# Depthwise convolution on tiles of the TensorE array, with channels copied across by GpSimd

## The chip, the cores and the metric

The kernel runs on one core of a Trainium2 chip. The metric is the device time of one execution in microseconds. [...] Each engine takes its instructions in the order of the program, so one that waits holds up all behind it on its engine.

## What is computed

Attention over a window of 32 positions to either side, for 8 batches of 8 heads with 576 positions and a head size of 64, and then a feed-forward part whose hidden layer gates itself by a convolution along the sequence.

```python
def _attn_ref(q, k, v):                      # (8, 8, 576, 64) each
    scores = scale * np.matmul(q, k.transpose(0, 1, 3, 2))
    mask = np.abs(pos[:, None] - pos[None, :]) <= 32
    scores = np.where(mask, scores, -1000000000.0)
    ...                                      # softmax
    return np.matmul(attn, v)

def _moe_ref(x, w_in, conv_w, w_out):        # x (8, 576, 512), w_in 512x1024, conv_w 3x1024
    h = np.maximum(x @ w_in, 0.0)
    hp = ...                                 # one row of zeros at either end of the sequence
    for k in range(3):
        conv_out += conv_w[k][None, None, :] * hp[:, k:k + S, :]
    gate = 1.0 / (1.0 + np.exp(-conv_out))
    return h * gate @ w_out                  # float32, (8, 576, 512)
```

The convolution is depthwise: each of the 1024 channels has three weights of its own and sees only itself.

## The kernel before

All matmul operands are bf16. The feed-forward part works with channels on partitions, in 12 chunks `c` of 384 positions (two thirds of a sequence) and 8 blocks `m` of 128 channels. For one block of one chunk the steps are: projection (`ph_mm`, 4 matmuls of 385 or so columns, the outer columns being the neighbours that the convolution needs), ReLU on ScalarE from PSUM into `hT` (`relu`), convolution, tanh on ScalarE in PSUM (`tanh`; the sigmoid is written with it), and the gate on VectorE (`gate`), which adds 1, multiplies by `hT` and writes `gT`. After a chunk's eight blocks come three groups of output matmuls (`py_mm`, 8 of 512 columns each), a copy on ScalarE and a store. Chunks 0 and 1 go in halves of 192 columns.

The convolution of a block is made in one of three ways, by tables (`ON_POOL`, `ON_DVE`, lines 1017 to 1029, `conv_by`). On TensorE (`pc_mm`) it is three matmuls, one a tap, with a 128x128 diagonal matrix of weights (`diag_w`) as the stationary operand and `hT` shifted by a column as the moving one; they add up in one PSUM bank. On VectorE (`conv_acc`) ScalarE makes the first tap into PSUM and VectorE adds the other two. On GpSimd (`conv_pool`) it is five operations in SBUF (`ca`, `cb`), and the tanh then reads SBUF. In chunks 2 to 11 the tables give 10 blocks to GpSimd, 43 to VectorE and 27 to TensorE.

The attention of batch `b` runs ahead of the chunks that need it. Per batch: loads of q, k, v in float32; casts to bf16 on GpSimd (`cast_qk`, `cast_v`); q and k turned so that the head dimension lies on partitions, by nine 128x128 transposes on TensorE for half of the heads (`tr_mm`, copied out of PSUM by ScalarE and VectorE in two parts), or, for q of the batches in `TURNED`, by a DMA transpose (`turn_q`, output `qT`); a copy of v shifted by 64 rows (`shift_v`, output `vo`, on VectorE or GpSimd by `VP`); scores for a pair of heads (`sc_mm`, 16 matmuls with 64 rows of the array, 64 columns; the ninth part of two pairs in `scl_mm`, 4 matmuls); exp on ScalarE; the mask on VectorE; attention times v (`av_mm`, 20 matmuls of 64 array columns and 65 moving columns); the division on VectorE; and a DMA transpose of the result into `xT`.

Nothing of this is written in its final order. `Planner` (lines 27 to 157) takes every operation with an engine, a due time (`want`), a duration, what it depends on, and what it takes and gives back: the 8 PSUM banks (`"p"`, one bank, or two neighbouring ones) and the buffers. It then simulates the engines and writes their instruction lists out: at each step, on each engine, among the operations that could start within 0.03 us of the earliest, the one with the least due time. The due times come from a chunk's start `chunk_at(c) = S2 + (c - 2) * PC`. The order is fixed when the kernel is built; on the chip each engine follows it, waiting where the real times are later than planned.

In the profile nearly all instructions show line 251, the helper that keeps program order. So groups go by the names of tiles: `pf` is PSUM, `xT,w_in_sb` the projection, `hT,diag_w` the convolution, `w_out_sb,gT` the output, `qT,kT` the scores, `ve,attn` and `vo,attn` attention times v, `ident,kb` and `ident,qb` the transposes.

Of the kernel before, what the change touches and what calls it, by code (L numbers as in the profile page):

```python
# [10 lines left out]
FP32 = mybir.dt.float32  # L11
# [5 lines left out]
class Op:  # L17
# [3 lines left out]
    def __init__(self, eng, want, dur, lat, fn, deps, takes, gives, dma, early, ring, shared):  # L21
        self.eng, self.want, self.dur, self.lat, self.fn, self.early = eng, want, dur, lat, fn, early
        self.ring, self.shared = ring, shared
        self.deps, self.takes, self.gives, self.dma = deps, takes, gives, dma


class Planner:
# [3 lines left out]
    def __init__(self, slots):  # L31
        self.ops = {}
# [3 lines left out]
    def add(self, key, eng, want, dur, fn, deps=(), lat=None, takes=(), gives=(), dma=None,  # L36
            early=0.0, ring="SP", shared=False):
        if lat is None:
            lat = {"ACT": 0.16, "DVE": 0.14, "POOL": 0.08}.get(eng, 0.12)
        assert key not in self.ops, key  # L40
        self.ops[key] = Op(eng, want, dur, lat, fn, deps, takes, gives, dma, early, ring,
                           shared or eng == "POOL")

    def run(self, fill, until):
# [14 lines left out]
        dma_free = 0.0  # L59
        port = {"DVE": 0.0, "POOL": 0.0}  # L60
        order = []

# [5 lines left out]
        def slots_at(op):  # L68
            at = 0.0
            for name, n in op.takes:  # L70
# [3 lines left out]
                if not pool:  # L74
                    return None
                at = max(at, pool[0][0])
            return at

        def take(name, n, start):
# [5 lines left out]
            ids = {i for _, i in pool}  # L85
            if name == "p":
                k = min(range(len(pool)), key=lambda k: (
                    max(pool[k][0], start), pool[k][1] ^ 1 in ids, pool[k][0]))
            else:
                k = 0  # L90
            return [pool.pop(k)[1]]

        done = 0
        while done < len(ops):
            best = None
            for e, now in engines.items():
# [8 lines left out]
                if not starts:  # L105
# [22 lines left out]
            engines[e] = start + op.dur  # L128
            end = start + op.dur + op.lat
# [5 lines left out]
            elif op.dma is not None:  # L135
                dma_free = max(dma_free, start + op.dur + 0.9) + op.dma
                end = dma_free + 0.9
            for name, of, k in op.gives:
# [22 lines left out]
def kernel(  # L161
# [30 lines left out]
    NCA = 3  # L192
# [32 lines left out]
    ca_pp = [pp.tile([128, CH], FP32, name=f"ca{i}") for i in range(NCA)]  # L225
    cb_pp = [pp.tile([128, CH], FP32, name=f"cb{i}") for i in range(2)]
    w_pp = [pp.tile([128, 1024], FP32, name=f"wst{i}") for i in range(4)]
# [7 lines left out]
    conv_w24 = pp.tile([3 * MB, 128], FP32, name="conv_w24")  # L235
    ident24 = pp.tile([3 * MB, 3 * MB], FP32, name="ident24")
# [51 lines left out]
    for t_ in ve_pp:  # L288
# [6 lines left out]

    plan = Planner({"p": range(8), "y": range(4), "ca": range(NCA), "cb": range(2),
                    "rec": range(6), "wst": range(4)})
# [10 lines left out]
    QK, V96, V128, WQ = 1.75, 0.9, 1.1, 1.7  # L308

    def load_qk(b, y, i):  # L310
        if b < BH:
            src = (q, k)[y][b, :, i * TH:(i + 1) * TH, :]
            for e in range(2):
                sync.dma_start(
                    qkst[y][i][:, e, :, :].rearrange("p j d -> p (j d)"),
                    bass.AP(src.tensor, src.offset + 4 * e * S * D, [[RP * D, 32], [S * D, 4], [1, RP * D]]),
                )
            return
# [24 lines left out]
    def turn_q(b, i):  # L343
        sync.dma_start_transpose(
            out=qT_sb[:, 2 * i:2 * i + 2, :].rearrange("p r (s x) -> p (r s) x", x=128),
            in_=qb_turn[b % 2][:, i].rearrange("p r s e d -> p (r s e d)"),
        )

    def load_v(b, c):
# [4 lines left out]
        )  # L354

# [818 lines left out]
```

## Time and profile before

| | |
|---|---|
| median of 3 runs (lowest, highest) | 222.89 us (221.91, 223.74) |
| profiled execution | 222.25 us |
| its span, first to last instruction | 220.4 us |
| granted TensorE clock | 1.00 |
| busy: PE, DVE, ACT, POOL | 208.4, 181.8, 187.7, 169.9 us |
| DMA | 48.28 MB, 219 GB/s over the span |

A row of the timeline has the start, the time from the first start to the last end, the engine, the operation, out<-in, rows*columns of the array that it uses, the shape, and how many instructions were merged into it. Matmuls overlap in the pipeline, so the second column of a TensorE row is longer than what the group costs the next; the distance between starts is the cost. Now and then a matmul's record is missing (a group of 8 shown as 7). A row of a group has the count, then busy time and the mean of one in ns, then the idle time ahead of them and what ended it. A row of windows has, for each engine, busy us and the count, then the clock, the share of time that the 16 DMA engines' packets took, and GB/s.

### The profile page before, as it was taken

The page shows a single profiled execution, that of the slowest core. Times are in us where ns is not written, and L with a number is a line of the kernel's source. Part 1 is how long each engine was busy: PE and PEld are TensorE (multiplying, and loading weights), DVE is VectorE, ACT ScalarE, POOL GpSimd, SP SyncE. Part 2 cuts the span into 40 slices and gives each one's busy share as a digit, 9 for nine tenths or more (in the row PEclk, how much of TensorE's full clock was granted, in tenths as well). Part 3 has the DMA queues.
Part 4 walks back from the last instruction along what each step waited for, and adds up shares of the span by engine and source line. Part 5 has one row for each costly group of instructions (what it writes and reads, how often), then busy time and mean ns, then how long its engine had stood idle before and what let it go on. Part 6 is the DMA issues. An engine that isn't in the chain of part 4 may idle for free.

```text
span 220.4 us, 6695 instructions
## 1 busy us (share of the span) xinstructions
PE 208.4 (95%) x2578; PEld 134.5 (61%) x2602; DVE 181.8 (83%) x361; ACT 187.7 (85%) x414; POOL 169.9 (77%) x204
## 2 busy tenths in 40 slices
PE   7898898999999988998999999999999999999993
PEld 7887797877666655554556555555565555545442
DVE  5388698997659999979898979969899989897930
ACT  3998698987797998699998898888999799999941
POOL 4663865787899999999799997789969449999600
PEclk9999999999999999999999999999999999999999
DMA  5999999996999999999999996999964325121123
GB/s 174 259 247 335 315 265 298 362 315 152 332 336 206 229 330 197 236 301 273 238 280 350 235 216 146 227 322 246 277 162 109 89 73 154 48 95 51 48 95 143
DMA packets 81667, 48.28 MB, mean 219 GB/s; under 512 B 64076, under 2 KB 69476, under 8 KB 81636
## 3 DMA queue, kind: packets, MB, share of 16 engines
q1 hardware_dynamic: 81600, 47.85, 85.4%
q8 instruction: 20, 0.33, 0.7%
q14 instruction: 11, 0.09, 0.1%
q10 hardware_dynamic: 36, 0.01, 0.0%
HBM read 32.52 MB, written 9.44 MB: 190 GB/s over the span
## 4 chain that ended last, share of the span: by engine, by line
PE 63%; DMA 11%; POOL 7%; ACT 6%; SPq 6%; DVE 4%; issue 3%; ACTq 0%; POOLq 0%
PE pf L251 63%; SPq L251 6%; DMA qT<-qb 4%; DMA vst<-in_v_dram 4%; POOL vo L251 3%; DMA wst<-in_moe_w_in_dram 3%; ACT pf L251 2%; ACT hT L251 2%; ACT attn L251 1%; POOL ve L251 1%; DVE attn L251 1%; DVE vo L251 1%; POOL w_in_sb L251 1%; ACT y L251 1%; DVE gT L251 1%
## 5 line engine op out<-in xcount | busy, mean ns | idle before, releaser
L251 PE MATMUL pf<-xT,w_in_sb 128*128 128x385 bf16 (+3 forms) x448 | 75.0, 305 | 2.6 <-POOL w_in_sb L251 0.8
L251 PE MATMUL pf<-w_out_sb,gT 128*128 128x512 bf16 (+1 forms) x272 | 66.1, 373 | 1.2
L251 DVE SCALAR_TENSOR_TENSOR gT<-pf,hT 128x384 bf16<-128x384 f32 (+1 forms) x112 | 52.7, 489 | 8.3 <-ACT pf L251 7.9
L251 PEld LDWEIGHTS <-w_in_sb 128*128 128x128 bf16 x448 | 40.5, 98 | 23.5 <-issue 2.0
L251 DVE SCALAR_TENSOR_TENSOR pf<-hT,conv_w_sb,pf 128x384 f32<-128x384 bf16 x86 | 51.6, 609 | 3.7 <-ACT pf L251 3.2
L251 ACT ACTIVATE hT<-pf 128x385 bf16<-128x385 f32 (+3 forms) x112 | 48.3, 462 | 3.7 <-PE pf L251 3.4
L251 ACT ACTIVATE pf<-pf 128x384 f32<-128x384 f32 (+1 forms) x102 | 43.6, 442 | 4.7 <-PE pf L251 3.2
L251 PEld LDWEIGHTS <-gT 128*128 128x128 bf16 x296 | 28.0, 98 | 28.7 <-issue 0.2
L251 ACT ACTIVATE attn<-pf 128x1024 bf16<-128x1024 f32 (+2 forms) x48 | 37.7, 816 | 0.4 <-PE pf L251 0.3
L251 POOL TENSOR_SCALAR vo<-ve 64x520 bf16<-64x520 bf16 x48 | 33.7, 702 | 3.7
L251 DVE TENSOR_TENSOR attn<-attn,mask 128x1152 bf16<-128x1152 bf16 (+2 forms) x32 | 29.3, 925 | 6.6 <-ACT attn L251 6.4
L251 ACT COPY y<-pf 128x512 f32<-128x512 f32 (+1 forms) x36 | 21.1, 585 | 13.0 <-PE pf L251 12.8
L251 POOL TENSOR_SCALAR ve<-vst 128x512 bf16<-128x512 f32 x40 | 26.6, 669 | 6.9 <-DMA vst<-in_v_dram 5.1
L251 PE MATMUL pf<-hT,diag_w 128*128 128x192 bf16 (+1 forms) x177 | 29.8, 283 | 0.2 <-ACT hT L251 0.2
L251 POOL TENSOR_SCALAR qb<-qst 128x512 bf16<-128x512 f32 (+1 forms) x22 | 19.7, 898 | 9.5 <-DMA qst<-in_q_dram 9.2
L251 DVE TENSOR_TENSOR xn<-pf,rec 128x640 bf16<-128x640 f32 (+1 forms) x34 | 26.3, 778 | 0.4
L251 ACT ACTIVATE pf<-hT,conv_w_sb 128x384 f32<-128x384 bf16 x43 | 25.5, 598 | 0.6 <-DVE xn L251 0.2
L251 POOL TENSOR_SCALAR cb<-hT,conv_w_sb 128x384 f32<-128x384 bf16 x20 | 25.1, 1259 | 0.2
L251 POOL TENSOR_SCALAR kb<-kst 128x1152 bf16<-128x1152 f32 x16 | 19.1, 1195 | 3.4 <-DMA kst<-in_k_dram 3.1
L251 POOL TENSOR_TENSOR ca<-ca,cb 128x384 f32<-128x384 f32 x20 | 20.2, 1019 | 0.5
L251 POOL TENSOR_SCALAR ca<-hT,conv_w_sb 128x384 f32<-128x384 bf16 x10 | 12.4, 1246 | 7.8 <-ACT hT L251 7.7
L251 PEld LDWEIGHTS <-diag_w 128*128 128x128 bf16 x177 | 14.6, 97 | 5.9 <-issue 0.6
(48 smaller groups left out, 227.9 us busy)
## 6 DMA issues: line engine op xcount, KB each, us to landing
out_dram<-y SPq DMA_DIRECT2D x35, 256.0 KB, 3.0
kst<-in_k_dram SPq DMA_DIRECT2D x12, 576.0 KB, 6.7
vst<-in_v_dram SPq DMA_DIRECT2D x24, 256.0 KB, 4.4
qst<-in_q_dram SPq DMA_DIRECT2D x6, 576.0 KB, 7.4
vst<-in_v_dram SPq DMA_DIRECT2D x16, 192.0 KB, 5.5
qst<-in_q_dram SPq DMA_DIRECT2D x6, 512.0 KB, 5.0
qst<-in_q_dram SPq DMA_DIRECT2D x8, 288.0 KB, 6.4
kst<-in_k_dram SPq DMA_DIRECT2D x8, 288.0 KB, 6.0
```

What stands on the lines that cost most here:

```text
L251: return lambda *args, **kwargs: fixed(do(*args, **kwargs))
```

## The change

The convolution on TensorE is made for several blocks at once in smaller tiles of the array. With 32x32 tiles, four blocks share the array. Rows 32i to 32i+31 serve block i alone and write to a PSUM bank of its own. The four column tiles of these rows make the four quarters of block i's 128 channels. A tile reads the 32 partitions that its rows stand on, so the other three quarters of the channels must first be copied to those partitions: GpSimd does it from `hT` to a buffer `hS`, three copies of 32 partitions for each block (`turn_part`). Each tap is then 16 matmuls on 16 tiles, 48 for four blocks (`pcn_mm`). With 64x64 tiles two blocks share the array in the same way: one copy for each, 12 matmuls. The small diagonal matrices that the moved channels need (`diag_off`) are built once, on VectorE, in the memory where the weights were staged.

```diff
+    NHS = 3
+    hS_pp = [pp.tile([128, 3, HR], BF16, name=f"hS{i}") for i in range(NHS)]
...
+    def turn_part(c, ms, i, x, s, engine):
+        n, w = len(ms), 128 // len(ms)
+        j = (i + 1 + x) % n
+        cols = hT_pp[c % 3].shape[2]
+        to, from_ = hS_pp[s][w * i:w * i + w, x, 0:cols], hT_pp[c % 3][w * j:w * j + w, ms[i], :]
...
+            cast_on(engine, to, from_)
+
+    def pcn_mm(c, ms, s, ps):
+        n, w = len(ms), 128 // len(ms)
+        step = HW + 2 if c % 3 == 1 else HW
+        dims = [[1, CH]] if step == HW else [[step, 2], [1, HW]]
+        for kk in range(3):
+            for x in range(-1, n - 1):
+                for i, m in enumerate(ms):
+                    rows, col = slice(w * i, w * i + w), (i + 1 + x) % n * w
+                    h_ = hT_pp[c % 3][rows, m, kk:kk + HW] if x < 0 else hS_pp[s][rows, x, kk:kk + HW]
+                    tensor.matmul(
+                        pf[ps[i]][col:col + w, 0:CH],
+                        diag_w[rows, kk, m, col:col + w] if x < 0 else diag_off[n][rows, x, kk, m, :],
+                        bass.AP(h_.tensor, h_.offset, [list(h_.ap[0])] + dims),
+                        start=(kk == 0), stop=(kk == 2),
+                    )
...
+    def make_diag_off(n, x):
+        to = diag_off[n][:, x].rearrange("p k m x -> p (k m) x")
+        w_ = conv_wr_sb[:, 1 if n == 2 else x].rearrange("p k m -> p (k m)")
+        vector.tensor_tensor(
+            out=to, in0=ident_in[n][:, None, :].broadcast_to([128, 3 * MB, 128 // n]),
+            in1=w_[:, :, None].broadcast_to([128, 3 * MB, 128 // n]), op=ALU.mult)
```

The tables are new. GpSimd makes no convolution any more, VectorE 40 blocks, TensorE 40: groups of four in chunks 2, 4, 5, 7, 8 and 9, groups of two in chunks 3 (two), 6, 10 and 11 (two), and four blocks alone (one each in chunks 2, 3, 4 and 11). All copies are on GpSimd (`HC`). A group takes four (or two) banks at once and is due `QGAP` after its last block.

```diff
-    ON_POOL = {2: (0,), 3: (), 4: (0,), 5: (0,), 6: (), 7: (0,), 8: (0,), 9: (0, 2), 10: (0, 2), 11: (0,)}
-    ON_DVE_2 = (1, 3, 4, 6)
...
+    QGAP, QGAP_N = 4.0, 3.5
+    ON_POOL_2 = ()
...
+    ON_DVE_2 = (1, 2, 5)
+    ON_DVE_3 = (2, 3, 6)
+    ON_DVE_4 = (1, 4, 7)
     ON_DVE_5 = (1, 3, 5, 6)
+    ON_DVE_6 = (1, 2, 3, 5, 6, 7)
+    ON_DVE_7 = (2, 3, 5, 6)
+    ON_DVE_8 = (2, 4, 5, 6)
+    ON_DVE_9 = (3, 4, 5, 7)
+    ON_DVE_10 = (0, 1, 3, 4, 5, 6)
+    ON_DVE_11 = (0, 1, 2)
...
+    TILED_2 = 4
+    TILED_3 = 2
...
+    HC = ("POOL", "POOL", "POOL")
...
+                            tq = at(group[-1]) + (QGAP_N if c == NCH - 1 else QGAP)
+                            hk = [("hc", c, group[0], i, x) for i in range(n) for x in range(n - 1)]
...
+                            add(ck, "PE", tq, 0.5 if n == 2 else 0.52,
...
+                                takes=[("p", -n)], gives=[("hs", hk[0], 0)])
```

Batches 4 and 5 have q and k transposed in 64x64 tiles, 36 transposes for half of the heads instead of nine, into two banks; batch 4's q no longer goes through the DMA transpose. Both copies out of PSUM stay, on VectorE and ScalarE.

```diff
+    def tr4_mm(b, y, i, ps):
+        nat = qkb_pp[b % 2][y][i]
+        for j in range(RP):
+            for e, r in ((0, 0), (1, 1), (1, 0), (0, 1)):
+                rows = slice(64 * r, 64 * r + 64)
+                tensor.transpose(
+                    pf[ps[r]][64 * e:64 * e + 64, :].bitcast(BF16)[:, 64 * j:64 * j + 64],
+                    nat[rows, j, e, :], ident[rows, 64 * r:64 * r + 64],
+                )
...
-    TURNED = (4, 6, 7)
+    TR4 = (4, 5)
+    TURNED = (6, 7)
```

The planner now knows shapes of tiles on TensorE. It charges `DRAIN` when the shape changes, and while TensorE is in a tiled shape (scores, attention times v, small transposes, grouped convolutions) it moves tiled work ahead as if due 3.0 us earlier. For one half of some batches it lets the first of two value groups wait for both masks (`AV_TOGETHER`). It also models how many descriptors the DMA ring holds.

```diff
+    MODES = {"sch": 1, "scl": 1, "sc": 1, "av": 2, "avc": 2, "tr4": 3, "pc2": 3, "pc4": 4}
+    DRAIN = 0.097
...
+        def gain(op):
+            if op.eng != "PE" or not mode or not op.mode:
+                return 0.0
+            return same if op.mode == mode else other
...
-                    key=lambda k: (ops[k].want, number[k]),
+                    key=lambda k: (ops[k].want - gain(ops[k]), number[k]),
                 )
+                if e == "PE" and ops[key].mode != mode:
+                    starts[key] = max(starts[key], now + self.DRAIN)
...
+    SAME, OTHER = 3.0, 3.0
```

The beginning is reworked. Batches 0 and 1 load and cast q and k in halves (`load_half`, `cast_half`), the very first casts on VectorE, ScalarE and GpSimd instead of GpSimd alone. The first load of v, and what follows on SP's queue, waits for the first half of q (`hold_back`: VectorE writes an element of `vst` after reading the loaded half). w_in is loaded as two of its four row blocks by 512 columns, so that blocks 0 to 3 need the first two loads. Half of the diagonals are built on VectorE. Batch 2's shifts of v move from GpSimd to VectorE.

```diff
+    def hold_back():
+        vector.tensor_copy(out=vst[96:97, 0, 0, 0:1], in_=qkst[0][0][96:97, 0, 0, 0:1])
...
-            src = moe_w_in.rearrange("(c p) f -> p c f", p=128)[:, :, 256 * x:256 * x + 256]
-            sync.dma_start(w_pp[s].rearrange("p (c f) -> p c f", c=KC), src)
+            src = moe_w_in.rearrange("(c p) f -> p c f", p=128)
+            c0, f0 = x % 2 * 2, x // 2 * 512
+            sync.dma_start(
+                w_pp[s].rearrange("p (c f) -> p c f", c=2), src[:, c0:c0 + 2, f0:f0 + 512])
...
+    W_BY = (("POOL", "POOL"), ("DVE", "ACT"), ("POOL", "POOL"), ("POOL", "POOL"))
+    CAST_BY = ('DVE', 'ACT', 'POOL', 'POOL')
-    HALF_AT = ((4.0, 16.0), (24.0, 30.0))
+    HALF_AT = ((6.0, 8.0), (24.0, 34.0))
-    LEAD = 18.0
+    LEAD = 8.0
+    DIAG_DVE = (0, 1, 2, 3)
-    VP = 2
+    VP = 3
-    PC = 14.2
-    S2 = 55.0
+    PC = 14.4
+    S2 = 54.5
```

Lists of two blocks (`ms`) for ReLU, tanh and gate are prepared for, but their tables (`PAIR_R`, `PAIR_G`) are empty, so these still work on one block at a time.

More of the change, by code (lines that the diff above doesn't have):

```diff
@@ L40, in add, with room, run @@
         assert key not in self.ops, key
+        by = self.shift.get(key[0], {})
+        want += by.get(key[1] if len(key) > 1 and isinstance(key[1], int) else None, 0.0)
         self.ops[key] = Op(eng, want, dur, lat, fn, deps, takes, gives, dma, early, ring,
[L42 to L44 removed]
+                           shared or eng == "POOL", self.MODES.get(key[0], 0), desc)
+    def room(self, t, own, flying):
+        while flying and flying[0][0] <= t:
+            flying.pop(0)
+        over = own - self.RING + sum(n * min(1.0, (f - t) / c) for f, c, n in flying)
+        for f, c, n in flying:
+            if over <= 0.0:
+                break
+            begin = max(t, f - c)
+            have = n * (f - begin) / c
+            t = begin + over * c / n if have >= over else f
+            over -= have
+        return t
+    def run(self, fill, until, same, other):
         ops = self.ops
@@ L838 @@
                 if w == 0:
-                    engine = ("DVE", "ACT")[half] if x == 0 else "POOL"
+                    engine = W_BY[x][half]
                 else:
```

545 lines of the change are left out of this document (365 added, 180 removed).

## Prediction

> **What bounds the kernel now.** I began with the table of windows, to see which engine has room in the long middle and in the part after the attention is done.
>
> ```profile
> core 0: us, PE busy (x) PEld busy (x) DVE busy (x) ACT busy (x) POOL busy (x), PEclk, DMA share, GB/s
> 55.00:160.00 105.00, 101.73 (x1235) 59.08 (x1250) 92.67 (x168) 92.95 (x187) 94.69 (x118) 1.00 1.12 262
> 160.00:213.00 53.00, 52.53 (x453) 28.48 (x457) 47.32 (x90) 48.44 (x106) 39.25 (x38) 1.00 0.32 90
> ```
>
> Every engine is near 90% in the middle, and after 160 us TensorE alone is full: GpSimd has 14 us free there. A busy TensorE need not be a packed one, so I read the chain of waits (start, length, what) next.
>
> ```profile
> 14.21 6.67 DMA wst<-in_moe_w_in_dram
> ...
> 20.95 1.78 POOL w_in_sb L251 x2
> ...
> 22.78 6.77 PE pf L251 x119
> ...
> 78.78 8.64 DMA vst<-in_v_dram
> ...
> 96.09 8.95 DMA qT<-qb
> ...
> 105.08 1.51 PE pf L251 x30
> ...
> 180.66 12.21 PE pf L251 x66
> ```
>
> Up to 22.8 us the loads and casts of w_in set the pace. From 73 to 105 us it runs through GpSimd's casts and shifts and two transfers; from 105 to 199 us it is TensorE alone. Whether TensorE is packed there shows in its timeline, by starts:
>
> ```profile
> 119.81 0.65 PE L251 MATMUL pf<-hT,diag_w 128*128 128x384 bf16 x3
> 120.30 0.82 PE L251 MATMUL pf<-xT,w_in_sb 128*128 128x385 bf16 x4
> 120.95 0.67 PE L251 MATMUL pf<-ident,kb 128*128 128x128 bf16 x9
> ...
> 123.93 0.22 PE L251 MATMUL pf<-ve,attn 128*64 128x65 bf16 x1
> ...
> 124.69 0.66 PE L251 MATMUL pf<-hT,diag_w 128*128 128x384 bf16 x3
> ...
> 128.59 0.41 PE L251 MATMUL pf<-qT,kT 64*128 64x64 bf16 x16
> 128.93 0.83 PE L251 MATMUL pf<-xT,w_in_sb 128*128 128x385 bf16 x4
> 129.69 0.41 PE L251 MATMUL pf<-qT,kT 64*128 64x64 bf16 x16
> 130.03 0.66 PE L251 MATMUL pf<-hT,diag_w 128*128 128x384 bf16 x3
> ...
> 133.24 0.22 PE L251 MATMUL pf<-ve,attn 128*64 128x65 bf16 x1
> ...
> 133.68 0.66 PE L251 MATMUL pf<-hT,diag_w 128*128 128x384 bf16 x3
> 134.27 0.22 PE L251 MATMUL pf<-ve,attn 128*64 128x65 bf16 x1
> ```
>
> Each group begins where the last one's columns end, so a group's cost is the distance between starts: a block's convolution 0.49 us (119.81 to 120.30), a projection of 4 matmuls 0.65. The same projection costs 0.76 when a group of another tile shape follows (128.93 to 129.69): a change of shape costs about 0.10 us, and the run is full of them. So TensorE's slots are the currency from 105 us on, and the sum below is made in them.
>
> **Convolution in tiles: −4.9 us.**
>
> ```profile
> L251 PE MATMUL pf<-hT,diag_w 128*128 128x384 bf16 x81 | 17.7, 327 | 0.2 <-ACT hT L251 0.2
> ```
>
> These 81 matmuls are 27 whole blocks; at 0.49 they fill 13.2 us. The new tables give VectorE 40 blocks instead of 43, GpSimd none instead of 10, and TensorE 40: six groups of four, six of two, four as before. A group of two is 12 matmuls on four 64x64 tiles: three rounds of 384 columns if the tiles run together, 0.49 us. A group of four is 48 matmuls on 16 tiles, also three rounds. What could keep it above 0.49 is the rate at which small matmuls start. The longest burst of them:
>
> ```profile
> L251 PE MATMUL pf<-ve,attn 128*64 128x65 bf16 x24 | 0.8, 196 | 0.0
> L251 PE MATMUL pf<-vo,attn 128*64 128x65 bf16 x16 | 0.8, 197 | 0.0
> ```
>
> These are the 40 from 123.93 to 124.69, 0.76 us; a group of 20 took 0.44 (133.24 to 133.68). So 20 more cost 0.32: 16 ns each, with a weight load each. At that rate 48 take 0.77 us. But four matmuls of 385 columns take 0.65 us (120.30 to 120.95), 0.42 ns a column, so 65 columns shared by two tiles need 14 ns anyway (65 x 0.42 / 2): 16 ns is mostly columns, not a floor. I take 0.55, near the lower end. New cost 6 x 0.55 + 6 x 0.50 + 4 x 0.49 = 8.3 us against 13.2: −4.9 (ends −5.3 and −3.6). [...]
>
> **Changes of shape for these groups: +1.8 us.** Twelve new groups in shapes of their own, one or two changes of 0.10 each: +1.2 to +2.4.
>
> **Transposes of batches 4 and 5: +1.5 us.** Batch 4's q comes off the DMA transpose; its k and batch 5's q and k go from nine transposes in 128x128 (9 x 128 columns at 0.42 ns, 0.49 us; six of these, 2.9 us) to 36 in 64x64, eight groups in all. By columns a group is a quarter of 36 x 64 x 0.42 ns = 0.24 us, by the 16 ns rate 0.58; I take 0.40, plus 0.10 to 0.20 for the change of shape: 8 x 0.55 = 4.4, so +1.5. Ends −0.2 and +3.3.
>
> **The planner joins groups of one shape: −1.6 us.** It now charges a change and, while in a tiled shape, pulls forward other tiled work. At 129 us one projection stands between two score groups, at 133.7 one convolution between two of attention times v; each such join saves two changes. With 24 score and 24 value groups after batch 1, all in twos would be 24 joins and −4.8, less those that stand together already (123.93). I take 8 joins; ends 0 and −4.8.
>
> **Stalls between 73 and 105 us: −1.5 us.**
>
> ```profile
> 78.51 0.39 PE L251 MATMUL pf<-qT,kT 64*128 64x64 bf16 x15 [0.58 <-DVE gT L251]
> ...
> 105.08 0.23 PE L251 MATMUL pf<-qT,kT 64*128 64x64 bf16 x4 [0.64 <-DMA qT<-qb]
> ```
>
> The second is batch 4's turned q, which the change takes off the queue: two of the six such transfers go, and with them their places on SP's queue, behind which the next loads stand. What is late next is batch 4's cast on GpSimd, then its copies out of PSUM. With others of the size of the first, about 3 us stand here; I take half, ends 0 and −3.
>
> **GpSimd: no gain on the path, and the main risk.**
>
> ```profile
> L251 POOL TENSOR_SCALAR cb<-hT,conv_w_sb 128x384 f32<-128x384 bf16 x20 | 25.1, 1259 | 0.2
> L251 POOL TENSOR_SCALAR kb<-kst 128x1152 bf16<-128x1152 f32 x16 | 19.1, 1195 | 3.4 <-DMA kst<-in_k_dram 3.1
> L251 POOL TENSOR_TENSOR ca<-ca,cb 128x384 f32<-128x384 f32 x20 | 20.2, 1019 | 0.5
> L251 POOL TENSOR_SCALAR ca<-hT,conv_w_sb 128x384 f32<-128x384 bf16 x10 | 12.4, 1246 | 7.8 <-ACT hT L251 7.7
> L251 POOL TENSOR_SCALAR qb<-qst 128x512 bf16<-128x512 f32 x12 | 7.4, 621 | 2.3 <-DMA qst<-in_q_dram 2.0
> ...
> L251 POOL TENSOR_SCALAR ca<-hT,conv_w_sb 128x384 f32<-128x384 bf16 x4 | 5.0, 1247 | 0.2 <-ACT hT L251 0.2
> ```
>
> Its convolutions go (25.1 + 20.2 + 12.4 = 57.7 us) and 84 copies of 386 columns come: 12 for a group of four, 2 for a group of two. Between 621 ns at 512 columns and 1195 at 1152 lies 0.9 ns a column over 162 ns, so a copy is about 0.51 us, 84 are 43 us. The total falls, but not where GpSimd is full: between 55 and 160 us (the last row is of that window) four of the ten convolutions go, 23 us, and the copies of chunks 2 to 7 come, four groups of four and three of two, 54 x 0.51 = 28 us, while batch 2's eight shifts of v (520 columns, 0.63 us each on the same line, 5 us) leave for VectorE. GpSimd stays at some 90% there. Behind a copy that waits for its ReLU stand the casts of the next batch, in order.
>
> **Extra VectorE work: +0.5 us.**
>
> ```profile
> L251 DVE TENSOR_TENSOR attn<-attn,mask 128x1152 bf16<-128x1152 bf16 x24 | 21.6, 913 | 4.9 <-ACT attn L251 4.8
> L251 DVE SCALAR_TENSOR_TENSOR pf<-hT,conv_w_sb,pf 128x384 f32<-128x384 bf16 x86 | 51.6, 609 | 3.7 <-ACT pf L251 3.2
> L251 DVE COPY vo<-ve 64x520 bf16<-64x520 bf16 x16 | 5.8, 364 | 1.7 <-POOL ve L251 1.3
> L251 DVE COPY qT<-pf 128x640 bf16<-128x640 bf16 x6 | 4.9, 819 | 0.2 <-ACT qT L251 0.2
> ```
>
> Three blocks fewer save 6 x 0.61 = 3.7 us. Batch 2's eight shifts of v (2.9), batch 4's q out of PSUM (1.6) and the off-diagonal weights come on: 1536 + 3 x 768 columns, at 913 ns for 1152 some 3.0 us. They fall between 35 and 70 us, where the first tiled chunk needs them; half the diagonals go to VectorE too, in the first 10 us. TensorE's slots hide most; uncovered they cost 3 us.
>
> **The start: −0.5 us.**
>
> ```profile
> 20.70 0.83 PE L251 MATMUL pf<-xT,w_in_sb 128*128 128x193 bf16 x8 [0.76 <-ACT attn L251]
> ...
> 3.43 3.34 SPq L251 DMA_DIRECT2D vst<-in_v_dram  x3
> ...
> 5.39 1.15 POOL L251 TENSOR_SCALAR qb<-qst 128x1152 bf16<-128x1152 f32 x1 [2.15 <-DMA qst<-in_q_dram]
> ```
>
> The first casts are halved and spread over three engines. Against it, the first load of v, and all on SP's queue behind it (second halves of q and k, w_in), waits until the first half of q has landed: between 0 and 2.0 us (3.43 to 5.39). w_in comes in rows twice as long, but four blocks now need two loads instead of one. The bytes ahead of the first projection (at 20.70) are the same or more, so I take little; ends −2.5 and +2.
>
> The tail keeps its form (a plain last block, then the output projection); due times carry no work. Sum: −4.9 + 1.8 + 1.5 − 1.6 − 1.5 + 0.5 − 0.5 = −4.7. The profiled execution took 222.25 us (220.4 span, 1.85 around it), 0.6 below the median of 222.89; 222.25 − 4.7 = 217.5 us, rounded.
>
> **Rivals.** *Copies come late, slower.* TensorE runs in order: a group of four that stands before its copies are done stops projections, scores and output behind it. It needs twelve copies, 6.1 us of GpSimd, where a convolution on GpSimd had about 8 us of slack by its due time and the group has 4. For it: 94.69 of 105 us busy. Against it: GpSimd sheds 57.7 us for 43 over the run. If the last three copies of each group come after its slot, 6 x 3 x 0.51 = 9 us: 227. It decides once more than half a group's copies trail the last ReLU. *ScalarE and VectorE become the bound.* Each is 88% busy (92.95 and 92.67 of 105), and four blocks arrive at once holding four of eight banks. Then the slots gained stay empty: 221.5. [...] *A floor on starts.* The 288 matmuls in groups of four and the 288 transposes stand at 11 ns each in my sum; each 10 ns more is 5.8 us. At 21 ns (16 scores in 0.34) the time is 223. [...] *The tiles do not all run together.* The trace shows two at a time. If it stays at two, a group of four costs 48 x 163/2 ns = 3.9 us and a group of two 0.98: some 240.
>
> **Numbers.** Forecast 0.63, ScalarE and VectorE 0.15, late copies 0.13, floor 0.06, two tiles 0.03. A measurement here tells 1% (2.2 us) from no change. Faster: nearly all of the forecast and a little of the second, 0.63. Within 1%: most of the second and parts of the floor and the late copies, 0.20. Slower: 0.17. Good ends of the joins, stalls and start together reach 211.5; the bad ends of transposes and VectorE with the second rival and the milder floor reach 224. The range 211.5 to 224 leaves out the late copies in full, the two tiles and some luck below.
>
> **What would show it.** Right: groups of four with 0.5 to 0.6 us between starts, fewer lone score groups, no idle TensorE before them. Wrong: TensorE idle before a group of four with GpSimd as the releaser (late copies); gaps released by gT or pf (second rival); a group of four over 0.8 us (floor) or over 2 us (two tiles). If the first projection starts later than 20.7 us, the start was mis-sized.

## The result, and the profile after

| | before | after |
|---|---|---|
| median (lowest, highest; runs), same chip | 222.49 us (221.91, 223.74; 4) | 241.34 us (240.83, 244.14; 4) |
| profiled execution, its span | 222.25, 220.4 us | 244.14, 242.0 us |
| granted TensorE clock | 1.000 | 0.979 |
| busy: PE, DVE, ACT, POOL | 208.4, 181.8, 187.7, 169.9 us | 216.3, 199.8, 188.8, 153.2 us |

In the profiles PE is TensorE and PEld its weight loads, DVE is VectorE, ACT ScalarE, POOL GpSimd and SP SyncE.

The ratio is 1.088, 95% interval 1.082 to 1.094: 19 us slower, where 217.5 was forecast. The profiled execution is the longest of the four, 2.8 us over their median. The windows that were shown of before, and one for the longer end (PE, PEld, DVE, ACT and POOL busy, clock, DMA share, GB/s):

```profile
55.00:160.00 105.00, 94.41 (x1600) 54.64 (x1599) 94.23 (x168) 87.01 (x175) 82.26 (x122) 1.00 0.90 227
160.00:213.00 53.00, 49.48 (x615) 26.62 (x613) 42.15 (x79) 42.10 (x87) 31.83 (x53) 0.94 0.53 115
213.00:242.00 29.00, 25.08 (x164) 12.99 (x162) 16.84 (x33) 19.86 (x45) 2.58 (x5) 1.00 0.22 82
```

In the middle TensorE was busy for 101.73 of 105 us and is now for 94.41. From 160 us, where it alone had been full, it has gaps and a lower clock. In the page's chain of what ended last, TensorE's share fell from 63% to 38% and VectorE's rose from 4% to 40% (before, then after):

```profile
PE 63%; DMA 11%; POOL 7%; ACT 6%; SPq 6%; DVE 4%; issue 3%; ACTq 0%; POOLq 0%
DVE 40%; PE 38%; ACT 8%; issue 7%; POOL 6%; POOLq 0%; ACTq 0%; DVEq 0%
```

Yet the grouped convolutions do what the forecast said. TensorE's timeline around a group of four, a group of two and a small transpose:

```profile
90.67 0.34 PE L306 MATMUL pf<-hT,diag_w 32*32 32x384 bf16 x4
90.68 0.37 PE L306 MATMUL pf<-hS,wst 32*32 32x384 bf16 x12
...
91.41 1.48 PE L306 MATMUL pf<-xT,w_in_sb 128*128 128x385 bf16 x8
...
96.84 0.35 PE L306 MATMUL pf<-hT,diag_w 64*64 64x384 bf16 x2
...
97.45 1.90 PE L306 MATMUL pf<-w_out_sb,gT 128*128 128x512 bf16 x8
...
117.08 0.48 PE L306 MATMUL pf<-ident,kb 64*64 64x64 bf16 x36
117.49 0.41 PE L306 MATMUL pf<-qT,kT 64*128 64x64 bf16 x16
```

From start to next start, a group of four takes 0.74 us (90.67 to 91.41) with its changes of shape, a group of two 0.61, the 36 small transposes 0.41. All 16 tiles run together: the 48 matmuls of 384 columns cost 0.74 us, where three of 384 columns on the whole array cost 0.49 in the kernel before. Four of the six groups of four took 0.74; the other two stopped inside, waiting (1.07 and 1.73). So where do 19 us come from? One row of windows from 24 us to the end, for before and for after:

```profile
24.00:220.40 196.40, 188.08 (x2226) 115.78 (x2247) 167.80 (x322) 169.61 (x373) 156.22 (x183) 1.00 0.85 214
```

```profile
24.00:242.00 218.00, 196.37 (x2807) 119.33 (x2804) 179.88 (x331) 173.06 (x376) 141.24 (x211) 0.98 0.75 190
```

The window is 21.6 us longer (218.0 against 196.4). TensorE's idle time in it rose from 8.3 (196.40 − 188.08) to 21.6 us: 13.3 of them. Of the 8.3 that busy time rose, the lower clock makes about 5 (an estimate, below). About 1 is work that now stands after 24 us: without dummy matmuls, TensorE was busy before 24 us for 6.5 us and is now for 5.6, since the first projection starts at 24.87 where it was 20.70. A part is only missing records (the trace of before has 272 of 296 output matmuls).

```profile
24.87 0.50 PE L306 MATMUL pf<-xT,w_in_sb 128*128 128x193 bf16 x4
```

Two stalls show how the gaps come about. In the first, four shifts of v for batch 1 (three of them in the row below), which were VectorE's before, too, now stand ahead of a gate whose PSUM bank the next projection needs (TensorE's rows, then VectorE's, then windows of 2 us):

```profile
48.16 0.41 PE L306 MATMUL pf<-hT,diag_w 128*128 128x192 bf16 x3
50.51 2.40 PE L306 MATMUL pf<-xT,w_in_sb 128*128 128x192 bf16 x16 [1.93 <-DVE gT L306]
52.70 0.69 PE L306 MATMUL pf<-hT,diag_w 128*128 128x192 bf16 x3
...
47.95 2.11 DVE L306 COPY vo<-ve 64x520 bf16<-64x520 bf16 x3
50.09 0.36 DVE L306 SCALAR_TENSOR_TENSOR gT<-pf,hT 128x192 bf16<-128x192 f32 x1
...
50.00:52.00 2.00, 1.50 (x12) 1.43 (x12) 1.97 (x3) 0.67 (x2) 1.71 (x2) 0.73 0.98 179
52.00:54.00 2.00, 2.00 (x15) 1.87 (x14) 1.54 (x5) 0.85 (x3) 2.00 (x3) 0.50 1.05 214
```

The three copies take 2.11 us, where one took 364 ns in the mean before; why they take longer here was not tested. The stall costs its 1.93 us and then more: the granted clock is 0.73 in 50 to 52 us and 0.50 in 52 to 54. The second stall comes from GpSimd and ScalarE (rows of GpSimd, ScalarE and TensorE, then windows):

```profile
170.41 5.13 POOL L306 TENSOR_SCALAR hS<-hT 32x388 bf16<-32x388 bf16 x9 [5.73 <-ACT hT L306]
...
181.78 2.18 POOL L306 TENSOR_SCALAR hS<-hT 32x388 bf16<-32x388 bf16 x3
184.04 1.00 POOL L306 TENSOR_SCALAR ve<-vst 128x512 bf16<-128x512 f32 x1
185.13 0.51 POOL L306 TENSOR_SCALAR hS<-hT 32x386 bf16<-32x386 bf16 x1
185.72 0.62 POOL L306 TENSOR_SCALAR vo<-ve 64x520 bf16<-64x520 bf16 x1
...
184.92 1.41 ACT L306 ACTIVATE attn<-pf 128x1024 bf16<-128x1024 f32 x2
...
183.81 0.39 PE L306 MATMUL pf<-qT,kT 64*128 64x64 bf16 x15 [0.54 <-ACT hT L306]
186.20 0.19 PE L306 MATMUL pf<-ve,attn 128*64 128x65 bf16 x1 [2.00 <-DVE pf L306]
...
186.00:188.00 2.00, 1.80 (x44) 1.12 (x44) 2.00 (x6) 1.47 (x5) 1.78 (x4) 0.86 0.03 8
188.00:192.00 4.00, 3.90 (x74) 2.13 (x74) 3.62 (x7) 2.88 (x5) 3.54 (x7) 0.64 0.44 82
```

The last shift of v of the last batch (at 185.72) stands behind 13 copies, nine of which waited 5.73 us for a ReLU. Attention times v needs it, and a bank that the first of ScalarE's two exps gives back at the same time. The profile names VectorE as the releaser; by the program's own dependencies it is these two (spans on GpSimd are rough). Here is the risk that the prediction named, work of the attention behind a copy that waits for its ReLU (it spoke of casts). But one such place is not the 19 us, so each suspect was tried.

### The profile page after: what moved, and what is told of

The parts are those of the page before. It is cut to its first block, busy times and chain, and to the rows that moved or that the text cites. A ratio compares the mean times of both kernels' runs of the same rounds, so it can differ in the third digit from the quotient of the medians.

```text
span 242.0 us, 7872 instructions
## 1 busy us (share of the span) xinstructions
PE 216.3 (89%) x3136; PEld 138.0 (57%) x3136; DVE 199.8 (83%) x388; ACT 188.8 (78%) x406; POOL 153.2 (63%) x232
## 4 chain that ended last, share of the span: by engine, by line
DVE 40%; PE 38%; ACT 8%; issue 7%; POOL 6%; POOLq 0%; ACTq 0%; DVEq 0%
PE pf L306 38%; DVE gT L306 7%; DVE pf L306 7%; DVE attn L306 6%; DVE xn L306 4%; DVE vo L306 3%; DVE kT L306 3%; ACT pf L306 3%; ACT attn L306 3%; DVE qT L306 2%; ACT hT L306 2%; DVE wst L306 2%; POOL hS L306 2%; POOL ve L306 2%; DVE diag_w L306 1%
## 5 line engine op out<-in xcount | busy, mean ns | idle before, releaser
L306 POOL TENSOR_SCALAR hS<-hT 32x386 bf16<-32x386 bf16 (+3 forms) x84 | 45.9, 547 | 38.3 <-ACT hT L306 32.4
L306 DVE SCALAR_TENSOR_TENSOR pf<-hT,conv_w_sb,pf 128x384 f32<-128x384 bf16 x80 | 47.2, 610 | 10.7 <-ACT pf L306 10.3
L306 ACT ACTIVATE pf<-pf 128x384 f32<-128x384 f32 (+1 forms) x112 | 45.9, 445 | 7.6 <-PE pf L306 5.3
L306 DVE TENSOR_TENSOR attn<-attn,mask 128x1152 bf16<-128x1152 bf16 (+2 forms) x32 | 31.4, 998 | 3.9 <-ACT attn L306 3.8
L306 POOL TENSOR_SCALAR ve<-vst 128x512 bf16<-128x512 f32 x40 | 29.0, 733 | 5.3 <-DMA vst<-in_v_dram 3.8
L306 POOL TENSOR_SCALAR kb<-kst 128x1152 bf16<-128x1152 f32 (+1 forms) x20 | 20.6, 1030 | 14.7 <-DMA kst<-in_k_dram 13.9
L306 POOL TENSOR_SCALAR vo<-ve 64x520 bf16<-64x520 bf16 x40 | 26.8, 670 | 2.9
L306 PE MATMUL pf<-hT,diag_w 128*128 128x192 bf16 (+3 forms) x216 | 23.8, 293 | 2.5 <-DVE gT L306 1.1
L306 POOL TENSOR_SCALAR qb<-qst 128x1152 bf16<-128x1152 f32 (+2 forms) x22 | 18.6, 854 | 7.3 <-DMA qst<-in_q_dram 4.5
L306 PE MATMUL pf<-qT,kT 64*128 64x64 bf16 x576 | 14.9, 194 | 5.7 <-DVE kT L306 3.1
L306 PEld LDWEIGHTS <-kT 64*128 64x128 bf16 x576 | 11.2, 96 | 13.9 <-issue 8.6
L306 PEld LDWEIGHTS <-attn 128*64 128x64 bf16 x640 | 13.1, 112 | 9.7 <-issue 5.3
```

Of the source, the lines that this page charges most:

```text
L306: return lambda *args, **kwargs: fixed(do(*args, **kwargs))
```

## The experiments

The first eight runs set three theories against each other. *Theory V*: VectorE's added work (diagonals, off-diagonal weights, shifts of v) makes TensorE late early on. *Theory T*: the grouped convolutions themselves cost it, by copies or by holding four PSUM banks. *Theory O*: the order that the planner now writes is worse. In the first five the order of the changed kernel is kept to the letter, and an operation is moved, replaced or dropped in its place. Kernels run together share their runs of the kernel before; ratios are to these.

**1. VectorE's additions on other engines.**

```diff
+        engine = "POOL" if b == 2 else engine
...
-        if engine == "ACT":
+        if True:
...
-        vector.tensor_tensor(
+        pool.tensor_tensor(
```

> The changed kernel, with its order of instructions kept; only what the change put on VectorE in the first 75 us is made elsewhere: half of the diagonals on ScalarE, the small identities, the off-diagonal weights and batch 2's shifts of v on GpSimd. Theory V (VectorE leads the first 100 us, and this extra work with the waits it meets there pushes everything back): some 14 us of VectorE work leaves a stretch that VectorE fills, so 229 to 233 us, VectorE's part of the chain of waits well under its 40%. Theory T (the grouped convolutions cost it: banks held, copies late): at most 2 us less, 239 or more.

Measured 246.69 us, 1.110 (1.092 to 1.128): no faster, and in its two runs slower still. Theory V expected 229 to 233. That the work costs more on GpSimd, in the places it has in this order, than it freed on VectorE is a reading, not shown; run 5 leaves GpSimd out of it.

**2. Grouped blocks convolved whole, no copies** (the copies go by the edit that run 3 shows).

```diff
...
+        for i, m in enumerate(ms):
+            pc_mm(c, m, None, ps[i:i + 1], (m,))
+        return
```

> The changed kernel, order kept; at each group's place the blocks are convolved one after another on the whole array (three matmuls each), and GpSimd's copies are left out. Theory V: TensorE has 10 us more work (six groups of four 1.2 us longer, six of two 0.4), partly into its idle time: 241 to 247. Theory T: the waits for copies go, 233 or less.

Measured 245.54, 1.105 (1.096 to 1.113): 4 us more than with the tiles and their copies, and 5.8 more than with the tiles and without copies (run 3, beside it on the same chip). In the same order the tiles help. This is not the −4.9 of the prediction's first term, which sets 40 blocks on TensorE against the 27 of before. Here 36 blocks change from whole to grouped, 17.6 us of slots (36 x 0.49) against 8.1 (6 x 0.74 + 6 x 0.61), so a little over half of the 9.5 us turned into time. Each group still takes its four or two banks at once in this run.

**3. The groups without GpSimd's copies** (`hS` set to zeros once).

```diff
...
-        if engine == "SP":
-            sync.dma_start(to, from_)
-        else:
-            cast_on(engine, to, from_)
+        return
```

> The changed kernel, order kept, without GpSimd's 84 copies (their buffers are zeroed once, so three quarters or half of each grouped block's channels are missing from the output). What the copies cost by their waits on TensorE and by their time on GpSimd goes, the tiles stay. Theory V: 239 to 241. Theory T in the form that copies come late: 233 or less.

Measured 239.77, 1.079 (1.068 to 1.089): 45.9 us of GpSimd's work gone, 1.6 us won, which is within the noise of the two ratios. Late copies are not the cause of the 19 us; at the one place looked at, the shift at 185.72, another wait (the exp) stands beside them.

**4. Runs 1 and 2 together.**

> Both edits at once: VectorE's extra work moved as in the first, plain convolutions without copies as in the second. Theory V: 230 to 238, TensorE's 10 us of extra work showing more than before because VectorE no longer hides it. Theory T: about as the second alone, 233 or less.

Measured 247.01, 1.111 (1.091 to 1.131): no better than either.

**5. VectorE's weights left out** (diagonals on ScalarE; small identities and off-diagonal matrices not built).

> The changed kernel, order kept; half of the diagonals back on ScalarE, and the small identities and the off-diagonal weights not built at all (the moved channels are multiplied by a piece of the ordinary diagonal matrices instead, so the grouped blocks' output is wrong). Unlike the run that moved this work, nothing is added to GpSimd. Theory V (VectorE's extra work in the first 75 us): the 5 us won by 60 us in that run stay to the end, 234 to 237. Theory O (the order that the planner now writes is worse wherever VectorE stands): within 2 us of 241.

Measured 240.82 and 245.02 us. No ratio stands on record for two runs so far apart; already the shorter one is only 0.5 us below the changed kernel, where theory V gave 234 to 237. Theory V falls as the whole cause. Theory T falls as far as copies and small matmuls go; that four banks are taken at once stays as it was in all five runs, so this part of it is not tested by them.

**6 to 8. One part undone, and the order written anew.** Run 6: no pulling together of shapes, and no value groups that wait for both masks. Run 7: transposes of batches 4 and 5 as before. Run 8: diagonals (engine and due time) and batch 2's shifts as before, and all of the first batch's shifts on VectorE again, half of which the change had put on ScalarE.

```diff
-    SAME, OTHER = 3.0, 3.0
+    SAME, OTHER = 0.0, 0.0
...
-    TR4 = (4, 5)
-    TURNED = (6, 7)
+    TR4 = ()
+    TURNED = (4, 6, 7)
-    XQ_AT = 2.0
+    XQ_AT = 0.0
...
-    DIAG_DVE = (0, 1, 2, 3)
+    DIAG_DVE = ()
-    VP = 3
+    VP = 2
```

> The changed kernel, planned anew without the pull towards work of the same tile shape and without value groups that wait for both masks. The whole order shifts, so this tells of the part and of a new order together. Theory O: the pull holds back projections and outputs whose time has come, so without it 5 us or more are gone, 236 or less, although the shape changes more often (over 140 times instead of 129). Theory V: 239 to 243.

> The changed kernel, planned anew with batches 4 and 5 turned as before (batch 4's q by DMA transpose, the rest in 128x128). Theory O, if these transposes are the place: 236 or less, and the stall between 100 and 110 us gone. Theory V: 1 to 2 us less for two copies out of PSUM fewer on VectorE, 239 to 242.

> The changed kernel, planned anew with the diagonals on ScalarE and due late as before, batch 2's shifts of v on GpSimd, and the first batch's on VectorE; the off-diagonal weights stay on VectorE. Theory V: 4 to 8 us less, 233 to 237. Theory O: anything, by the new order; within 3 us of 241 if VectorE's part doesn't matter.

Measured 235.03 (ratio 1.056), 237.06 (1.065) and 236.32 (1.061). Three parts that have little to do with each other, and each is worth 4 to 6 us (5 to 7 by the ratios). Run 6 came out as theory O said and run 8 as theory V said; run 7 lies between the two. Either each part really costs that, or any new order is better than this one.

**9 and 10. The mask left out, in after and in before.** *Theory E*: VectorE empties the PSUM banks too late.

> The changed kernel in its own order, without the multiplications by the mask on VectorE (the softmax keeps what lies outside the window, so the output is another one): some 60 operations of about 0.99 us, 55 to 60 us of VectorE's 199.8, go. Theory E (TensorE waits because VectorE empties the PSUM banks too late, and in the changed kernel VectorE stands at 14.2 to 15.0 of 15 us through most of the middle): the time falls by 8 us or more, to 233 or less. Theory O (the order itself, fixed over all engines, makes TensorE wait, whatever VectorE's load): the time falls by less than 3 us.

> The kernel before in its own order, without the multiplications by the mask (the output is another one). Both theories: TensorE was packed before, so little is won, 0 to 3 us; 219 to 223. If it falls by as much as the changed kernel does, the mask tells nothing about the change.

Measured 236.46 (1.057, 1.045 to 1.069), 4.9 below the changed kernel (some 7 by the ratios, 1.088 and 1.057), and 220.67 (0.986, 0.979 to 0.993), about 3 below before. The masks are 32 operations and 31.4 us in the changed kernel, not the 60 and 55 to 60 of the expectation. With a sixth of VectorE's work off, 2 to 4 us more are won than before wins by it. That lies between what theories E and O gave, and leaves most of the 19 us to something else than VectorE's load.

**11 and 12. Parts of the change put on the kernel before.** *Theory G*: the groups cost it. *Theory R*: the rest does. Run 11 adds the tile groups to the kernel before (its planner, start, loads and pace kept). Run 12 has no tiles, only the changed kernel's numbers for start, loads and pace:

```diff
-    HALF_AT = ((4.0, 16.0), (24.0, 30.0))
-    FF_AT = (13.0, 24.0, 38.0)
+    HALF_AT = ((6.0, 8.0), (24.0, 34.0))
+    FF_AT = (17.0, 24.0, 35.0)
...
-    LEAD = 18.0
+    LEAD = 8.0
...
-    PC = 14.2
-    S2 = 55.0
+    PC = 14.4
+    S2 = 54.5
```

> The kernel before with the convolution in 64x64 and 32x32 tiles alone: the groups, GpSimd's copies, the off-diagonal weights and the table of blocks on VectorE as in the changed kernel; its start, its loads' times, its transposes, its planner and its pace as before. Theory G (the groups cost it: four banks held at once, copies, weights): 233 or more. Theory R (the rest of the change, start, loads, joined shapes, transposes, costs it): 224 or less. Between them both have a part.

> The kernel before with the changed kernel's numbers for its start, its pace and its loads alone (loads due 8 us ahead where it was 18, the first parts at the later times, the chunks 14.4 us apart); no tiles. Theory R: 229 or more, since these numbers bring part of the loss without the tiles. Theory G: 225 or less.

Measured 235.48 (1.053, 1.045 to 1.061) and 230.16 (1.029, 1.018 to 1.040). Both lose, 12 and 7 us, as theory G said of run 11 and theory R of run 12; so neither theory is the whole. Run 12 is telling: its planned operations stand on the same engines as in the kernel before, and only numbers in the planner differ. So does any other order lose?

**13 to 15. The same operations in another order.** Run 15 changes one number of the kernel before:

```diff
-    MO, ME = 7.0, 9.0
+    MO, ME = 6.38, 9.0
```

Runs 13 and 14 keep the operations of the changed kernel and of run 11. Their pace numbers were moved in small steps, some thousand times, and the order kept that the kernel's own planner counts shortest. Run 13:

```diff
-    LEAD = 8.0
+    LEAD = 7.35
...
-    MO, ME = 7.0, 9.0
+    MO, ME = 7.50, 9.12
...
-    PC = 14.4
-    S2 = 54.5
+    PC = 14.32
+    S2 = 54.66
...
-    HC_AT = 1.0
+    HC_AT = 1.70
...
-    QGAP, QGAP_N = 4.0, 3.5
+    QGAP, QGAP_N = 3.60, 3.49
```

> The changed kernel, every operation of it on the same engine, with another written-out order: the pace numbers alone moved in small steps (chunks 14.32 us apart for 14.4, loads due 7.35 us ahead for 8, attention 7.5 us ahead of its chunk for 7.0, groups due 3.6 us behind their projections for 4.0, GpSimd's copies 0.7 us later), chosen among some thousand such draws as the order that the kernel's own planner counts shortest. Theory O (the loss is the order that the planner happened to write for the change): the time falls by 8 us or more, to 233 or less. Theory G (the operations themselves cost it: banks, copies, VectorE's additions): within 3 us of the changed kernel, 238 to 244.

> The kernel before with the tile groups alone (as in the run with the tiles only, 235.48 us), with the pace numbers moved in small steps and chosen in the same way. Theory O: 225 or less, near the kernel before, since the tiles were only given a bad order. Theory G: 232 or more.

> The kernel before with one number moved: the odd sequences' attention is due 6.38 us ahead of its chunk where it was 7.0; no operation is added, removed or moved to another engine, but the planner writes another order. Theory O: 225 us or more, so the kernel before stands on a chosen order and a mere new draw costs microseconds. Theory G: 221 to 224, within 1% of the kernel before.

| | us | ratio to before (95%) |
|---|---|---|
| changed kernel, redrawn | 231.69 | 1.039 (1.033 to 1.046) |
| tiles alone, redrawn | 228.17 | 1.024 (1.021 to 1.027) |
| before, one number moved | 229.38 | 1.029 (1.026 to 1.031) |

The changed kernel gets 9.6 us back without losing an operation, and the kernel before loses 6.4 without gaining one. Theory O is shown for about half of the loss: a new order alone is worth 6 to 10 us here. Run 14 met neither theory; it lies between them. The row of windows from 24 us of the changed kernel redrawn, and of before with one number moved:

```profile
24.00:229.70 205.70, 189.26 (x2763) 114.13 (x2785) 177.87 (x330) 170.23 (x374) 142.47 (x211) 1.00 0.81 204
```

```profile
24.00:227.70 203.70, 190.76 (x2232) 118.20 (x2254) 170.27 (x322) 170.17 (x373) 157.30 (x183) 0.99 0.81 205
```

Redrawn, TensorE's idle time falls from 21.6 to 16.4 us and the clock is full again. In the kernel before, the moved number raises it from 8.3 to 12.9 us. From the changed kernel to its redraw, the busy times of VectorE, ScalarE and GpSimd change by 1 to 3 us (179.88 to 177.87, 173.06 to 170.23, 141.24 to 142.47); what changes is how they lie to each other.

The planner's own count tells a part of this without the chip. Its plan, which is made when the kernel is built, ends at 214.2 us for the kernel before and at 219.4 for run 15, and at 224.0 for the changed kernel and 212.7 for its redraw. So some 10 of the 19 us stood in the changed kernel's plan before anything ran. The plan does not hold the rest: the kernel before takes 8.3 us more than its plan, the changed kernel 17.3 and its redraw 19.0. The two planners count with other durations, so the changed kernel's plans and those of before compare only roughly.

**16 to 18. Equal treatment for before.** Run 16 redraws the kernel before as run 14 redrew the tiles. For runs 17 and 18 the planner also got durations nearer to the traces, and could move blocks between VectorE and TensorE and choose the size of groups, for the kernel before and for the tiles alike.

> The kernel before, every operation on the same engine, with its pace numbers moved in small steps and chosen as the order that its own planner counts shortest: the same treatment that the tiles and the changed kernel got. Theory O (what is left of the loss after a new draw is the lack of the choice that the kernel before has behind it): 225 to 230, level with the tiles' 228.17. Theory G (what is left are the operations): 220 to 224, so that the tiles stand 2% behind at equal treatment.

> The kernel before with the planner's durations brought nearer to the traces (mask 1.0 us, shifts 0.38 and 0.68, casts 1.2 and 0.72, some 0.03 more for each operation of ScalarE and VectorE), then pace numbers and the table of VectorE's blocks drawn anew. It is the partner of the next run. Theory O: 220 to 226.

> The kernel before with tile groups alone, with the same durations in the planner, the pace, the table of VectorE's blocks and the size of the groups by chunk drawn anew (groups of two in some chunks, whole blocks in others). Theory O: level with its partner to within 1.5%, 221 to 227, since the tiles' TensorE time and GpSimd's lighter load stand against VectorE's additions. Theory G: 3 us or more behind its partner.

Measured 222.51 (1.004, 0.999 to 1.008), 232.05 (1.046, 1.034 to 1.057) and 231.71 (1.041, 1.031 to 1.052). The search keeps the kernel before where it was, and brings the tiles to 5.7 us of it. That is what theory G said of run 16: at this treatment the tiles stand some 2% behind. With the fitted planner both are equal, as theory O said, but both are bad, where 220 to 227 was expected. So that TensorE's savings turn into time in some order, or that tiles cost in every order, is not settled; no order was found here in which the tiles beat the kernel before.

## Why the prediction was wrong

**The step that failed** is "So TensorE's slots are the currency from 105 us on, and the sum below is made in them". It holds while the order stays as it is and TensorE stands packed in it. This change makes the planner write the whole order anew, and in the new one TensorE is not packed: its idle time from 24 us rose by 13.3 us, and its clock fell. The slots of the convolutions and transposes came out near the sum (below) and did not decide; the terms for joins, stalls and start failed with the order. What stood in its place is worth, by the runs, 9.6 us for the drawn order alone (run 13; some 11 by the ratios). The cause of the other 9 stays open, between the tiles, the rest of the change and their order: the tiles redrawn stand 2.4% above the runs of before beside them, where before redrawn stands level. Four banks taken at once, VectorE's added work and a search that was too short were not told apart.

Term by term:

- *Convolution in tiles and its changes of shape, −4.9 + 1.8.* Right as slots. With their changes groups were to cost 0.65 to 0.75 us (four) and 0.60 to 0.70 (two); they took 0.74 and 0.61. With four whole blocks that is 10.1 us against 13.2, the −3.1 of the forecast, without the stops inside two groups (1.07 and 1.73 us from start to next start).
- *Floor on starts.* Excluded, at the 21 ns that 223 was priced with: the 48 matmuls of the group at 90.67, neighbours on different tiles, start within 0.48 us, 10 ns apart.
- *Transposes, +1.5.* Too high: 0.41 us with the change of shape between two score groups (117.08 to 117.49), where 0.55 was taken; eight of them come to some 3.3 us against 2.9 before.
- *Joined shapes, −1.6.* Met as a count, open as a price. The trace has 129 changes of shape where before had 126, so the joins did hold back what the new groups add. But pulling tiled work ahead is one of the things that set the new order. Without it the kernel runs 6 us faster (run 6), and a new draw alone can also give that, so whether the pull itself costs time is not shown.
- *Stalls from 73 to 105 us, −1.5.* Wrong. The wait for batch 4's turned q (0.64 us) went, and others took its place (0.93 us at 75.38, 0.56 at 79.30, 0.45 at 101.47).
- *GpSimd, no gain, and late copies as a rival (227).* The copies took 546 ns for 0.51 forecast, 45.9 us in all for 43. The rival's picture is right in places (the shift at 185.72), its price is not: 1.6 us without any copy (run 3). The sign that was named for it, TensorE idle before a group until GpSimd is done, does not stand among the waits of the changed kernel.

```profile
POOL hS L306 <- ACT hT L306: 32.4, 6, 11.5
```

In this row of the waits GpSimd waits 32.4 us at the head of copies, 11.5 at the longest, with casts behind. A long wait of an engine still is no price; the run without it is.

- *VectorE, +0.5.* Mis-sized as work: its busy time rose by 18 us, where the priced operations come to some 4 (−3.7 + 2.9 + 1.6 + 3.0) and the diagonals have no price. A part of it is the same operations taking longer:

```profile
L306 DVE TENSOR_TENSOR attn<-attn,mask 128x1152 bf16<-128x1152 bf16 x24 | 23.2, 990 | 2.6 <-ACT attn L306 2.5
L306 DVE COPY vo<-ve 64x520 bf16<-64x520 bf16 x20 | 9.7, 483 | 0.5
L306 DVE TENSOR_SCALAR diag_w<-ident,conv_w_sb 128x128 bf16<-128x128 bf16 x12 | 4.1, 401 | 0.0
L306 DVE TENSOR_TENSOR wst<-ident,conv_wr_sb 128x768 bf16<-128x768 bf16 x3 | 3.6, 1235 | 0.0
```

A shift took 483 ns for 364, a mask 990 for 913, and the off-diagonal weights 5.3 us (3.6, and 1.7 for the wide one) for 3.0. But leaving the weights out, with the diagonals on ScalarE, gave nothing (run 5).

- *Start, −0.5.* Wrong in sign: the first projection came 4.2 us later, outside the end of +2 that was given. On SP's queue the first load of v, and all behind it, begins at 5.03 us where it was 3.43:

```profile
2.15 1.24 SPq L306 DMA_DIRECT2D kst<-in_k_dram  x2
5.03 1.57 SPq L306 DMA_DIRECT2D vst<-in_v_dram  x3
```

The numbers for start, loads and pace alone, without this hold, already cost the kernel before 7 us (run 12).

- *The second rival, VectorE and ScalarE as the bound (221.5).* Its sign in the profile came, gaps released by `gT` and `pf`, and VectorE at 40% of the chain. It was priced as slots that stay empty, no slower than before, and 221.5 is given without its sum. With the masks gone VectorE's work fell by a sixth for 2 to 4 us more than the same brings before (runs 9 and 10), so it has a share, and a small one.

No rival was "another order with more stalls". The forecast took the range's upper end from the bad ends of single terms; run 15 puts the price of a mere new order at 6.4 us, more than its whole sum of −4.7. The length of the changed kernel's own plan, 10 us over that of before, was there to be read and has no term in the sum.

## What to carry to other kernels

Where a planner or a list scheduler writes the order of all engines, a change of any input draws a new order, and the spread between draws belongs into the forecast before any saving does: one moved due time cost this kernel 2.9%. Read first what the planner itself counts for the new order. Before a local change is judged, draw the order anew for both kernels in the same way and compare the best of each. And when the bounding engine is packed only thanks to a chosen order, count what a change saves on it as an opening, not as time.

## What the hardware did that was not expected

Stalls here cost more than themselves. After 2.00 us without work, following 0.54, the granted clock was 0.86 in 186 to 188 us and 0.64 in 188 to 192; eight matmuls of the projection took 2.41 us from start to start (188.78 to 191.19) where the same eight took 1.41 at 181.60. The profiled execution of the changed kernel has three such dips (from 50.91, 160.13 and 187.44 us), each a clock of 0.50 for 3.41 us, some 5 us together (an estimate: half of the 10.2 us that the dips last). The profiled executions of the kernel before and of the redrawn one have none, with mean clocks of 1.000; mean clocks of 0.992 and 0.993 in others of their runs fit one dip each, since half of 3.41 us is 0.7 to 0.8% of their spans. Between the dips the clock is full for 105.81 and 23.89 us. The longest gaps in TensorE's work in the 3.41 us ahead of the three were 1.93, 0.59 and 2.00 us. What the dips share is little work in those 3.41 us. These are the windows ahead of each dip and in it:

```profile
47.50:50.91 3.41, 1.29 (x22) 1.12 (x15) 3.30 (x6) 2.40 (x7) 2.67 (x4) 1.00 1.30 204
50.91:54.32 3.41, 3.41 (x26) 3.21 (x24) 2.82 (x5) 1.55 (x5) 3.41 (x4) 0.50 0.93 199
...
156.72:160.13 3.41, 1.78 (x56) 1.37 (x50) 3.36 (x7) 2.50 (x5) 3.12 (x6) 1.00 1.09 369
160.13:163.55 3.42, 3.30 (x47) 1.92 (x45) 3.42 (x7) 2.26 (x4) 3.20 (x4) 0.50 1.38 236
...
184.03:187.44 3.41, 1.41 (x55) 1.14 (x48) 3.41 (x9) 3.41 (x8) 3.09 (x5) 1.00 0.18 35
187.44:190.85 3.41, 3.31 (x26) 1.61 (x25) 3.41 (x6) 2.12 (x5) 2.95 (x7) 0.50 0.23 44
```

TensorE was busy for 0.38, 0.52 and 0.41 of the three windows ahead. Whether that is what brings the dips was not tested.
